# A mixture of experts behind attention and an MLP: products grouped by weight part, later table writes, another seam

## The chip, the cores and the metric

The kernel runs on one core of one Trainium2 chip. The metric is the device time of one execution in microseconds. TensorE is PE in the rows (PEld are its weight loads), VectorE is DVE, ScalarE is ACT, GpSimd is POOL and SyncE is SP.

## What is computed

The reference, cut to what matters. B is 4, 12 heads, 448 positions, 64 per head; x has 1792 rows of 768.

```python
scores = cap * np.tanh((q @ k.T * scale) / cap)
attn = softmax(scores) @ v                         # x: 1792 x 768
h = x @ w_in                                       # 768 -> 2048
x = (h * sigmoid(h)) @ w_out                       # 2048 -> 768
do = x @ w_skip > 0                                # rows that meet an expert
e = argmax(x[do] @ w_gate)                         # one of 8
y[e] = gate_w * (np.maximum(x[e] @ w1[e], 0) @ w2[e])   # 768 -> 1024 -> 768
out = x; out[do] = x[do] + y
```

## The kernel before

All products run in fp32 halves: a number is cut into a high part h and a low part l, and a product is the sum of hi·hi, hi·lo and lo·hi. A high part is a cast on ScalarE, a low part a subtraction on VectorE (or POOL).

Attention fills the first 200 us and the dense MLP the time to about 681; the change does not touch them. Then comes the tail, which is laid out by hand: engines issue in the order in which the Python code records their instructions, and every engine works its own list in order.

The tail begins with the router of the last batch and `group()`, which finds the most loaded expert. Two blocks of few tokens, `fu` and `fv`, have been chosen ahead; their products (`f_h`, `f_y`, L1100) use a quarter of TensorE's columns each and no halves. `f_add` (L1139) sums them on VectorE, `s3_out` (L1077) scatters rows to the output by an indirect DMA on POOL.

The most loaded expert is then worked in blocks of 128 tokens, `gs[0]` to `gs[3]`. For these inputs there are three: block 0 and block 1 are full, and block 2 is "small" (at most 64 rows, where the two halves of the low products share one pass). They share one set of weights. A block is:

- `ids_load` (L889): a DMA reads its 128 token numbers from `table` in DRAM. `own_ids` (L804, L805) corrects the numbers for the last batch, so that blocks 0 and 1 need not wait for the table scatters.
- `x_gather` (L895): an indirect DMA on POOL gathers its rows of x.
- `x_turn` (L972): six transposes on TensorE; `x_split` (L986, L987) cuts the result into halves.
- `h_mm` (L1008): 36 products with w1 (6 parts of the depth, 2 halves of the width, 3 kinds). `h_relu` (L1020), `h_turn` (L1030, L1037, L1038) transpose and cut h.
- `s3_y` (L1051): 48 products with w2; `s3_add` (L1070) adds on VectorE; `s3_out`.

Weights come in six pieces, w1 in three of two rows (1024 columns each) and w2 in three of three, three and two rows (768 columns each). `w_load` (L928) loads a piece on SP, `w_split` and `row_split` (L942, L943) cut it, and `w_next` loads the next expert's piece into the buffer that has come free.

Behind the group come the listed blocks: `cur` and `nxt_`, whose experts, places and number come from `block_list` on VectorE (L811 to L859). `cur` is worked in `body`, the last in `few_body`. Which way the program goes is decided by branches on a register, one for each engine: `more` (L1518), `last` (L1512).

`route_c` scatters the table of token numbers for a batch: four indirect DMAs on POOL (L690). In the kernel before it stands ahead of the gather of block 1, and SP's loads of the later ids wait for it.

The seam is the end of the last group block, where the weights of `cur` must be cut while the block's own y products run. In the kernel before ScalarE casts its pieces (L1481, L942, L1495), VectorE cuts rows 0 to 2, POOL row 3 (L943), and rows 4 and 5 follow the sums; three products of `cur` stand ahead of the branch (`cur.begun = 1`), the rest in `body`.

Of the kernel before, what the change touches and what calls it, by code (L numbers as in the profile page):

```python
# [17 lines left out]
P = 128  # L18
# [4 lines left out]
DM = 768  # L23
# [40 lines left out]
def kernel(  # L64
# [810 lines left out]
    def s_who(idx, re=None):  # L875
        u = Blk()
        u.idx = idx
        u.w1, u.w2, u.raw = {}, {}, {}
        u.begun = 0
        u.small, u.q = False, 1  # L880
        if re is not None:
            u.er = nc.sync.value_load(re, min_val=0, max_val=E - 1)
        return u
# [102 lines left out]
            nc.scalar.copy(h, px)  # L986
            nc.vector.tensor_tensor(l, px, h, op=ALU.subtract)  # L987

    def few(o, t, k, n, h, l):
        both = (o, t[:, k * P : (k + 1) * P], h)  # L990
        rest = (o[:HP], t[:, k * P : k * P + HP], l)
        for i, (o_, t_, w_) in enumerate((both, rest) if k < n - 1 else (rest, both)):
            nc.tensor.matmul(o_, t_, w_, start=(k == 0 and i == 0), stop=(k == n - 1 and i == 1))

    def h_mm(u, nh, ds):
        if nh == 0 and ds[0] == 0:
# [4 lines left out]
        for d in ds:  # L1001
            h, l = u.w1[d]
            o = nh * 512
            if u.small:
                few(u.ph[nh], u.xTh, d, ND, h[:, o : o + 512], l[:, o : o + 512])
                continue
            for x_, w_, st in ((u.xTh, h, 0), (u.xTh, l, 1), (u.xTl, h, 2)):
                nc.tensor.matmul(  # L1008
                    u.ph[nh],
                    x_[:, d * P : (d + 1) * P],  # L1010
                    w_[:, o : o + 512],
                    start=(d == 0 and st == 0),
                    stop=(d == ND - 1 and st == 2),
                )

    def h_relu(u, nh):
        if u.small:
# [22 lines left out]
    def s3_y(u, fs, nhs=(0, 1)):  # L1040
        if 0 in fs:
            u.py = [bank(f"py{nh}") for nh in range(2)]
        for f in fs:
            h, l = u.w2[f]
            for nh in nhs:
                o = nh * HO
                if u.small:
                    few(u.py[nh][:, :HO], u.hTh, f, NF2, h[:, o : o + HO], l[:, o : o + HO])
                    continue
                for x_, w_, st in ((u.hTh, h, 0), (u.hTh, l, 1), (u.hTl, h, 2)):  # L1050
                    nc.tensor.matmul(  # L1051
                        u.py[nh][:, :HO],
                        x_[:, f * P : (f + 1) * P],
                        w_[:, o : o + HO],
                        start=(f == 0 and st == 0),
                        stop=(f == NF2 - 1 and st == 2),
                    )

    def y_out(u):
        i = u.idx % 2  # L1060
# [48 lines left out]
    def f_h(u, ph, ds):  # L1109
        u.ph = ph  # L1110
        r = P // u.q
        for d in ds:
            f_mm(u, ph, u.xT[:, d * r : (d + 1) * r], w_row(u, 1, d), F2, d == 0, d == ND - 1)
# [232 lines left out]
            w_split(u, which, k, eng=nc.gpsimd if (which, k) in ((1, 1), (2, 2)) else nc.vector)  # L1346
            w_next(near, u, which, k)

    def hidden(u, mid=None, mid2=None, both=0):
        h_mm(u, 0, range(u.begun, both or ND))  # L1350
        if both:
            h_mm(u, 1, range(both))
            h_mm(u, 0, range(both, ND))
        h_relu(u, 0)
        if mid is not None:
            mid()
        h_mm(u, 1, range(both, 4))
        h_turn(u, 0)
        if mid2 is not None:
            mid2()  # L1360
        h_mm(u, 1, range(4, ND))
        h_relu(u, 1)

    fu, fv = ahead
# [27 lines left out]
    g0 = s_who(0, regsg[:, :1])  # L1392
    for k in range(3):
        w_load(g0, 1, k)
    w_load(g0, 2, 0)
# [9 lines left out]
    for i in (0, 1):  # L1405
        nc.scalar.copy(w_tile(1, 0, "h")[:, i * F2 : (i + 1) * F2], w_row(g0, 1, i))
    f_relu(fv)
    for k in (1, 2):
        w_load(g0, 2, k)
    py = [ps_y.tile([P, 512], F32, tag="py", name=f"pyf{i}") for i in range(2)]  # L1410
    f_y(fu, py[0], range(6))
    f_hturn(fv, ps_m.tile([P, 512], F32, tag="pm", name="ptf1"), hTf[1:])
    f_y(fu, py[0], (6, 7))
    block_list(*blocks())
    route_c(B - 1)
    own_ids(1, gids[1])
    x_gather(gs[1], xg[1])
    f_add(fu)
    s3_out(fu)
    for i in (0, 1):  # L1420
        row_split(g0, i, done=True)
    for i in (2, 3):
        nc.scalar.copy(w_tile(1, 1, "h")[:, (i - 2) * F2 : (i - 1) * F2], w_row(g0, 1, i))
    f_y(fv, py[1], range(6))
    x_turn(g0)
    f_y(fv, py[1], (6, 7))
    x_split(g0)
    for i in (2, 3):
        row_split(g0, i, done=True)
    for i in (4, 5):  # L1430
        row_split(g0, i)
    w_split(g0, 2, 0)
    f_add(fv)
    s3_out(fv)
    for i in range(2, NG):
        gs.append(ids_load(s_who(i), regsg[:, 1 + i : 2 + i], gids[i]))
    x_gather(gs[2], xg[2])
    total = nc.sync.value_load(regt, min_val=1, max_val=MAXB)

    def listed(i):  # L1440
        u = s_who(i + 1, regs[:, i : i + 1])
        u.real = total > i
        return ids_load(u, regs[:, MAXB + i : MAXB + i + 1], ring["ids"][(i + 2) % 3])

    cur = listed(0)
    x_gather(cur, xg[0])
    w_load(cur, 1, 0)
    for k in range(3):
        w_next((cur,), g0, 1, k)
    w_next((cur,), g0, 2, 0)  # L1450
    nxt_ = listed(1)
# [3 lines left out]
    ng = nc.values_load(regsg[:, 1 + NG :], min_val=0, max_val=2 * NG + 1)  # L1455

    def group_block(i, end, small=False):
# [8 lines left out]
        if end and i != 1:  # L1466
            x_gather(nxt_, xg[1])

        def mid():
            nc.scalar.copy(w_tile(2, 1, "h"), w_raw(g0, 2, 1))  # L1470

        def mid2():
            w_split(u, 2, 1, done=True)
            w_next(pair, g0, 2, 1)

        if i:
            hidden(u)
        else:
            hidden(u, mid, mid2, 2)
        if end:  # L1480
            nc.scalar.copy(w_tile(1, 0, "h"), w_raw(cur, 1, 0))  # L1481
        x_turn(nxt)
        s3_y(u, (0,))
        h_turn(u, 1)
        if i == 0:
            w_split(u, 2, 2)
            w_next(pair, g0, 2, 2)
        x_split(nxt)
        if end:
            w_split(cur, 1, 0, done=True)  # L1490
            w_next(pair, cur, 1, 0)
            row_split(cur, 2)
            row_split(cur, 3, nc.gpsimd)
            w_next(pair, cur, 1, 1)
            nc.scalar.copy(w_tile(1, 2, "h"), w_raw(cur, 1, 2))  # L1495
        s3_y(u, range(1, 4))
        for nh in range(2):
            s3_y(u, range(4, NF2), (nh,))
            s3_add(u, nh)
        if end:  # L1500
            for d in (4, 5):
                row_split(cur, d, done=True)
            w_next(pair, cur, 1, 2)
            h_mm(cur, 0, range(1))
            cur.begun = 1
        s3_out(u)
        if end and i == 1:
            x_gather(nxt_, xg[1])

    def more(i):  # L1510
        def last():
            with tc.If(ng == 2 * i + 3) as half:  # L1512
                group_block(i, True, True)
            with half.Else():
                group_block(i, True)

        if i + 1 < NG:
            with tc.If(ng > 2 * i + 3) as branch:  # L1518
                group_block(i, False)
                if i == 0:  # L1520
                    x_gather(gs[3], xg[3])
                more(i + 1)
            with branch.Else():
                last()
        else:
            last()
# [4 lines left out]
    def body(u, v, alike):  # L1531
# [167 lines left out]
```

## Time and profile before

| what | us |
|---|---|
| three runs: median, lowest, highest | 811.39, 807.75, 1092.96 |
| the profiled execution | 808.66 |
| its span, first to last instruction | 806.9 |
| TensorE matmul busy | 780.7 (97%) |
| VectorE, ScalarE, POOL busy | 471.5, 419.6, 318.0 |
| TensorE's mean granted clock | 0.987 |

A row of a timeline gives the start, the length, the engine, the line, the operation and its operands, and in brackets how long the engine had been idle and what ended that. Line numbers are those of the kernel before. Matmul records overlap: the time of one is read from the distance of two starts. The clock is a share of the full 2.4 GHz.

### The profile page before, as it was taken

Reading aid. Unit: us, or ns where it says so; the run is one execution under the profiler, and the core shown is the slowest. Engines: PE = TensorE matmul, PEld = TensorE weight load, DVE = VectorE, ACT = ScalarE, POOL = GpSimd, SP = SyncE. Lnnn points to the kernel's source line nnn. Section 1 sums busy time; section 2 is a strip of 40 time slices with the busy share of each in tenths; the row PEclk is TensorE's granted clock in tenths of the full one; section 3 lists DMA queues with packets and bytes.
Section 4 is the critical chain, followed back from the end, with each engine's and each line's share of the span. In section 5 each row is a group of like instructions: output and inputs, shape, how many; then the busy total and the mean of one; then the engine's idle time right before and its main releaser. Section 6 shows DMA issues by size and latency. Waiting matters only on the chain. (4 is left out here: it accounts for less than half of the span.)

```text
span 806.9 us, 11338 instructions
## 1 busy us (share of the span) xinstructions
PE 780.7 (97%) x4082; PEld 580.9 (72%) x4082; DVE 471.5 (58%) x678; ACT 419.6 (52%) x584; POOL 318.0 (39%) x218
## 2 busy tenths in 40 slices
PE   7998999999999999999999999999999999899895
PEld 2222222237899999989898999988999896579773
DVE  2799888778888864435424674333664332582451
ACT  6997999993566654443433443333454221252520
POOL 3698988875655545455530220000100000231250
PEclk9999999999999999999999999999999999889998
DMA  7332333341777645677754436965465752876270
GB/s 247 112 131 69 104 116 126 116 149 37 210 209 211 197 130 157 192 221 207 209 171 152 113 101 240 294 208 166 122 207 165 218 144 91 310 257 254 77 242 22
DMA packets 78090, 135.24 MB, mean 168 GB/s; under 512 B 8630, under 2 KB 47926, under 8 KB 78018
## 3 DMA queue, kind: packets, MB, share of 16 engines
q1 hardware_dynamic: 76226, 130.34, 52.0%
q0 software_dynamic: 1504, 4.00, 1.6%
q8 instruction: 38, 0.62, 0.3%
q14 instruction: 34, 0.28, 0.1%
q10 hardware_dynamic: 288, 0.00, 0.0%
HBM read 108.17 MB, written 31.01 MB: 172 GB/s over the span
## 5 line engine op out<-in xcount | busy, mean ns | idle before, releaser
L508 PE MATMUL ph<-x,whi 128*128 128x448 f32 x768 | 217.8, 365 | 0.1
L508 PEld LDWEIGHTS ph<-x,whi 128*128 128x128 f32 x768 | 143.1, 188 | 13.9 <-issue 2.9
L533 PE MATMUL py<-gh,who 128*128 128x448 f32 x384 | 143.3, 373 | 0.0
L533 PE MATMUL py<-gh,wlo 128*128 128x448 f32 x384 | 141.0, 367 | 0.0
L508 PE MATMUL ph<-x,wli 128*128 128x448 f32 x384 | 139.5, 363 | 1.5 <-POOL wli L432 1.5
L533 PE MATMUL py<-gl,who 128*128 128x448 f32 x384 | 140.8, 367 | 0.0
L244 ACT ACTIVATE a<-a,capt 128x896 f32<-128x896 f32 x84 | 87.6, 1043 | 2.8
L243 ACT ACTIVATE a<-psc,tsc 128x896 f32<-128x896 f32 x84 | 83.4, 993 | 8.1 <-PE psc L147 6.1
L204 DVE RECIPROCAL rd<-pden 128x448 f32<-128x448 f32 x24 | 70.9, 2953 | 23.7 <-PE pden L200 23.7
L429 ACT CAST who<-wro 128x512 fp32r<-128x512 f32 x72 | 44.7, 621 | 73.0 <-PE py L533 66.2
L533 PEld LDWEIGHTS py<-gh,who 128*128 128x128 f32 x384 | 72.1, 188 | 10.6 <-ACT who L429 2.2
L525 DVE TENSOR_TENSOR gl<-scr_e,gh 128x448 fp32r<-128x448 f32 x64 | 55.4, 865 | 40.7 <-ACT gh L523 40.0
L523 ACT CAST gh<-scr_e 128x448 fp32r<-128x448 f32 x64 | 36.3, 568 | 80.4 <-DVE scr_e L520 80.4
L533 PEld LDWEIGHTS py<-gh,wlo 128*128 128x128 f32 x384 | 72.1, 188 | 7.1 <-DVE wlo L432 0.4
L508 PEld LDWEIGHTS ph<-x,wli 128*128 128x128 f32 x384 | 72.0, 188 | 6.9 <-POOL wli L432 1.9
L533 PEld LDWEIGHTS py<-gl,who 128*128 128x128 f32 x384 | 72.2, 188 | 6.2
L147 PE MATMUL psc<-q,k 64*128 64x448 f32 x288 | 71.0, 593 | 4.7 <-DMA q<-in_q_dram 4.1
L690 POOL DMA_INDIRECT table<-slotd,si x16 | 17.7, 1107 | 141.9 <-DVE si L680 138.0
L163 POOL TENSOR_TENSOR sm<-sm,a 64x448 f32<-64x448 f32 x48 | 60.4, 1260 | 17.0 <-DVE sm L151 14.6
L176 PE MATMUL pav<-a,vt 128*64 128x448 f32 x288 | 64.6, 562 | 0.0
L432 DVE TENSOR_TENSOR wlo<-wro,who 128x512 fp32r<-128x512 f32 x48 | 33.1, 690 | 53.0 <-ACT who L429 51.1
L154 POOL TENSOR_TENSOR sm<-sm,a 128x896 f32<-128x896 f32 x24 | 51.5, 2145 | 22.1 <-DVE sm L151 10.9
(279 smaller groups left out, 1118.3 us busy)
## 6 DMA issues: line engine op xcount, KB each, us to landing
raw64i<-in_moe_w_in_dram SPq DMA_DIRECT2D x16, 768.0 KB, 5.2
raw64o<-in_moe_w_out_dram SPq DMA_DIRECT2D x24, 512.0 KB, 4.1
wri<-ws_in SPq DMA_DIRECT2D x32, 384.0 KB, 3.1
wro<-ws_out SPq DMA_DIRECT2D x48, 256.0 KB, 3.8
xs<-scr_xo SPq DMA_DIRECT2D x36, 224.0 KB, 4.9
s<-in_moe_w_dram SPq DMA_DIRECT2D x7, 1024.0 KB
ws_in<-wri SPq DMA_DIRECT2D x16, 384.0 KB, 5.7
ws_out<-wro SPq DMA_DIRECT2D x24, 256.0 KB, 4.8
```

What stands on the lines that cost most here:

```text
L147: nc.tensor.matmul(psc[:, j, :S], self.k[r, c * P : (c + 1) * P], self.q[r, :], start=True, stop=True)
L154: nc.gpsimd.tensor_tensor(self.sm, self.sm, self.a[2], op=ALU.add)
L163: nc.gpsimd.tensor_tensor(self.sm[r, q_], self.sm[r, q_], rest[r, o : o + S], op=ALU.add)
L176: nc.tensor.matmul(self.pav[r, :S], self.vt[:, c * 2 + j, :], self.a[c][:, q_], start=(c == 0 and self.hp % 2 == 0), stop=(c == KF - 1 and ...
L204: nc.vector.reciprocal(rd, self.pden[:, :S])
L243: nc.scalar.activation(a.rearrange("p (j s) -> p j s", j=2), self.psc[:, :, :S], AF.Tanh, scale=tsc)
L244: nc.scalar.activation(a, a, AF.Exp, scale=capt)
L429: nc.scalar.copy(self.wh[:, :w], self.wr[:, :w])
L508: nc.tensor.matmul(ph, w_[:, c * P : (c + 1) * P], x_[b, c], start=(n == 0), stop=(n == 3 * ND - 1))
L523: nc.scalar.copy(h, e)
L525: nc.vector.tensor_tensor(l, e, h, op=ALU.subtract)
L533: nc.tensor.matmul(py[:, :S], w_[:, c * P : (c + 1) * P], g_, start=(hf + c + st == 0), stop=(hf == NQ - 1 and c == QC - 1 and st == 2),)
```

## The change

In plain words:

1. `few` becomes `products`, and `h_mm` and `s3_y` take the kinds of products as an argument: "h" for hi·hi, "x" for the low part of the tokens, "l" for the low part of the weights. The products of a block are as many as before; they now run grouped by kind.
2. In front of block 0, its ids are loaded on SP ahead of all but one register load, then the first weight piece, then the ids of block 1; a value that POOL writes behind the gather of block 0 (`gate`) holds back the other five pieces on SP. The list of blocks is made earlier on VectorE.
3. Block 0's h products are issued ahead of the branch, with the cuts of rows 2 to 5 between them; the transposes of block 1's x follow.
4. The table scatters, the loads of the later ids and the gathers of block 2 and of `cur` move behind block 0's h products, all onto POOL (`late_ids`). SP no longer waits for the scatters.
5. `first_block` gives block 0 an order of its own for the w2 cuts and the y products.
6. At the seam ScalarE casts all of w1, VectorE cuts rows 0 and 1 ahead of the sums and rows 2 to 5 in `body` (`late`), POOL cuts none, and eight hi·hi products stand ahead of the branch (`cur.begun = 4`).

```diff
+    def products(small, o, th, tl, ks, n, parts, w_of_k):
+        for part in parts:
+            for k in ks:
+                h, l = w_of_k(k)
+                if not small:
+                    t, w_ = {"h": (th, h), "x": (tl, h), "l": (th, l)}[part]
+                    mms = [(o, t[:, k * P : (k + 1) * P], w_)]
+                else:
+                    both = (o, th[:, k * P : (k + 1) * P], h)
+                    rest = (o[:HP], th[:, k * P : k * P + HP], l)
+                    mms = {"h": [both] if k < n - 1 else [], "x": [], "l": [rest] if k < n - 1 else [rest, both]}[part]
...
-    def hidden(u, mid=None, mid2=None, both=0):
-        h_mm(u, 0, range(u.begun, both or ND))
+    def hidden(u, mid=None, mid2=None):
+        for nh in range(2):
+            h_mm(u, nh, range(u.begun, ND), "h")
+        h_mm(u, 0, range(ND), "x")
+        early = bool(u.small or u.late)
+        if early:
+            h_mm(u, 1, range(ND), "x")
+        h_mm(u, 0, range(ND), "l")
         h_relu(u, 0)
...
-    gs = [ids_load(g0, regsg[:, 1:2], gids[0], nc.scalar)]
-    gs.append(ids_load(s_who(1), regsg[:, 2:3], gids[1], nc.scalar))
+    ids_load(g0, regsg[:, 1:2], gids[0])
+    g0.er = nc.sync.value_load(regsg[:, :1], min_val=0, max_val=E - 1)
+    w_load(g0, 1, 0)
+    ids_load(gs[1], regsg[:, 2:3], gids[1])
...
+    gate = const.tile([1, 1], I32, name="gate")
+    nc.gpsimd.memset(gate, 0)
+    nc.sync.value_load(gate, min_val=0, max_val=0)
...
-    block_list(*blocks())
-    route_c(B - 1)
-    own_ids(1, gids[1])
-    x_gather(gs[1], xg[1])
-    f_add(fu)
+    block_list(*blocks())
+    for d in (0, 1):
+        row_split(g0, d, done=True)
+    f_add(fu)
+    f_y(fv, py[1], range(4))
+    x_turn(g0)
+    f_y(fv, py[1], range(4, NF2))
+    x_split(g0)
+    own_ids(1, gids[1])
+    x_gather(gs[1], xg[1])
...
+    for nh in range(2):
+        h_mm(g0, nh, (0, 1), "h")
+    for nh in range(2):
+        h_mm(g0, nh, (0, 1), "lx")
...
+    h_mm(g0, 1, (4, 5), "l")
+    nc.scalar.copy(h2[:, :DM], w_row(g0, 2, 0))
+    h_relu(g0, 1)
+    f_add(fv)
+    s3_out(fv)
+    x_turn(gs[1])
...
+    def first_block(end):
+        h_turn(u, 1)
+        nc.scalar.copy(h2[:, DM:], w_raw(u, 2, 0)[:, DM:])
+        for nh in range(2):
+            s3_y(u, range(3), (nh,), "hx")
+        w_cut(w_raw(u, 2, 0), h2, l2, done=True)
...
+    def late_ids(end):
+        route_c(B - 1)
+        if not end:
+            for i in range(2, NG):
+                ids_load(gs[i], regsg[:, 1 + i : 2 + i], gids[i], nc.gpsimd)
+            x_gather(gs[2], xg[2])
+        listed(0, cur, nc.gpsimd)
+        x_gather(cur, xg[0])
+        listed(1, nxt_, nc.gpsimd)
...
         if end:
-            w_split(cur, 1, 0, done=True)
+            for k in (1, 2):
+                nc.scalar.copy(w_tile(1, k, "h"), w_raw(cur, 1, k))
+            for d in (0, 1):
+                row_split(cur, d, done=True)
             w_next(pair, cur, 1, 0)
-            row_split(cur, 2)
-            row_split(cur, 3, nc.gpsimd)
...
-            h_mm(cur, 0, range(1))
-            cur.begun = 1
+            cur.begun, cur.late = 4, range(2, ND)
+            for nh in range(2):
+                h_mm(cur, nh, range(cur.begun), "h")
...
+        for d in u.late:
+            row_split(u, d, done=True)
+            if d % 2:
+                w_next(near, u, 1, d // 2)
         splits(u, 2, (0,), near)
```

On SP, in front of block 0: before, the six weight pieces (L928; `s`, `r` and `xraw` are buffers) stand behind one register load, and the ids loads of blocks 0 and 1 stand on ScalarE's queue.

```order
L882 TENSOR_LOAD regsg
L882 ISA x2
L928 ISA
L928 DMA s_5804<-in_moe_w_dram 128x2x1024
L928 ISA
L928 DMA r_4042<-in_moe_w_dram 128x2x1024
```

The same place in the changed kernel:

```order
L889 DMA idg_5924<-table 128x2
L1391 TENSOR_LOAD regsg
L1391 ISA x2
L928 ISA
L928 DMA s_5804<-in_moe_w_dram 128x2x1024
L887 TENSOR_LOAD regsg
L887 ISA x2
L889 ISA
L889 DMA idg_5925<-table 128x2
L1402 TENSOR_LOAD gate
L1402 ISA x2
L928 ISA
```

Two ids loads have come ahead of the weights, and the read of `gate` stands between the first piece and the other five.

On POOL, from the gather of block 0 (`idg_5924`) on, as a difference (`table` is what `route_c` writes, the stores to `out_dram` are those of fu and fv):

```order
 L895 DMA scr_xo<-xs,idg_5924 128x768
+L1401 MEMSET gate 1x1
+L895 DMA xraw<-xs,idg_5925 128x768
+L1070 DMA out_dram<-scr_xt,ids_4037 1792x768
+L1070 DMA out_dram<-scr_xt,ids_4038 1792x768
+L1465 TENSOR_LOAD regsg
+L1559 COMPARE_AND_BRANCH
 L690 DMA table<-slotd,si_5885 15360x2 x4
-L895 DMA xraw<-xs,idg_5925 128x768
-L1077 DMA out_dram<-scr_xt,ids_4037 1792x768
-L1077 DMA out_dram<-scr_xt,ids_4038 1792x768
```

The four scatters have moved behind the gather of block 1, both stores and the branch; behind them now stand, on POOL too, the ids loads of blocks 2 and 3 and then the gather of block 2.

On ScalarE, from the second cut of x of block 0 to its w2 casts (`h_0` and so on are high parts of a piece, `xTh` and `hTh` those of x and h). Before:

```order
L986 CAST xTh_6139<-px_9_5531 128x256
L942 CAST h_2_18_6148<-r_4043 128x1024 x2
L942 CAST h_0_20_6154<-r_4044 128x2304
L1455 TENSOR_LOAD regsg
L1518 COMPARE_AND_BRANCH
L1020 ACTIVATE scr_e<-ph_g 128x512
L1470 CAST h_1_24_6291<-xraw 128x2304
L1037 CAST hTh_6264<-pt_g 128x512
L1020 ACTIVATE scr_e<-ph_g 128x512
L1037 CAST hTh_6264<-pt_g 128x512
L942 CAST h_2_26_6333<-xraw 128x1536
```

In the changed kernel:

```order
L942 CAST h_2_20_6198<-r_4043 128x1024 x2
L1024 ACTIVATE scr_e<-ph_g 128x512
L1041 CAST hTh_6168<-pt_g 128x512
L1457 CAST h_0_22_6232<-r_4044 128x768
L1024 ACTIVATE scr_e<-ph_g 128x512
L1465 TENSOR_LOAD regsg
L1559 COMPARE_AND_BRANCH
L1041 CAST hTh_6168<-pt_g 128x512
L1474 CAST h_0_22_6232<-r_4044 128x1536
L942 CAST h_1_24_6346<-xraw 128x2304
L942 CAST h_2_26_6351<-xraw 128x1536
```

The first w2 piece is cast in two parts, the second of them behind the second cast of h, and the other two pieces follow that.

## Rows read from the trace of the kernel before

**Rows 1.** Stretches: PE, PEld, DVE, ACT, POOL busy us (instructions), granted clock, DMA share, GB/s.

```profile
580.00:600.00 20.00, 20.00 (x102) 18.77 (x101) 13.90 (x34) 10.51 (x17) 5.38 (x5) 1.00 0.52 163
680.00:700.00 20.00, 18.49 (x196) 11.32 (x194) 8.92 (x53) 4.27 (x8) 0.87 (x1) 0.83 0.69 242
700.00:720.00 20.00, 16.95 (x125) 10.78 (x122) 16.61 (x33) 8.43 (x10) 7.78 (x7) 0.83 0.79 255
720.00:740.00 20.00, 20.00 (x110) 18.05 (x109) 9.05 (x11) 6.25 (x10) 6.26 (x5) 1.00 0.98 382
760.00:780.00 20.00, 16.81 (x81) 13.67 (x80) 16.93 (x13) 11.25 (x10) 13.55 (x4) 0.91 0.68 228
```

**Rows 2.** Timeline of PE: start, us, line, out<-in, count, idle before.

```profile
701.64 1.59 PE L1100 MATMUL pyf<-l,hTl 128*32 128x192 f32 x24 [0.43 <-ACT hTl L1125]
...
712.21 0.80 PE L1008 MATMUL ph_g<-h,xTh 128*128 128x512 f32 x1
...
731.08 0.39 PE L1008 MATMUL ph_g<-h,xTh 128*128 128x512 f32 x1
...
739.71 0.82 PE L972 MATMUL px<-ident,xg 128*128 128x128 f32 x6
```

**Rows 3.** Waits, 680 to 714: engine line <- released by: us, times, longest.

```profile
PEld pyf L1100 <- issue: 5.8, 9, 1.3
...
DVE idg L804 <- DMA idg<-table: 5.5, 1, 5.5
```

**Rows 4.** Timeline of POOL.

```profile
699.13 1.04 POOL L895 DMA_INDIRECT scr_xo<-xs,idg  x1 [104.28 <-DMA idg<-table]
...
704.27 0.95 POOL L690 DMA_INDIRECT table<-slotd,si  x1 [0.30 <-issue]
...
733.51 1.03 POOL L895 DMA_INDIRECT scr_xo<-xs,idg  x1 [0.30 <-issue]
...
751.58 1.03 POOL L895 DMA_INDIRECT xraw<-xs,ids  x1 [0.30 <-PE ph_g L993]
```

**Rows 5.** Timeline of PE at the seam.

```profile
767.35 0.49 PE L1008 MATMUL ph_g<-h,xTh 128*128 128x512 f32 x1 [3.07 <-DVE scr_xt L1070]
...
768.58 0.63 PE L1008 MATMUL ph_g<-l,xTh 128*128 128x512 f32 x1
...
772.01 0.39 PE L1008 MATMUL ph_g<-l,xTh 128*128 128x512 f32 x1
```

**Rows 6.** Line L1512 on the engines' queues: ns min/median/max, first and last start.

```profile
L1512 PEldq COMPARE_BRANCH  x2: 83/1852/3622, 749.5 to 763.0; - x2
```

**Rows 7.** Timeline of ACT.

```profile
773.22 1.47 ACT L942 CAST h<-xraw 128x1536 fp32r<-128x1536 f32 x1
```

**Rows 8.** Timeline of DVE, and the POOL row beside its last.

```profile
706.40 1.69 DVE L1139 SCALAR_TENSOR_TENSOR scr_xt<-pyf,ids,xg 32x192 f32<-32x192 f32 x4 [2.02 <-remote]
...
721.73 0.69 DVE L1038 TENSOR_TENSOR hTl<-pt_g,hTh 128x512 fp32r<-128x512 f32 x1 [1.04 <-ACT hTh L1037]
...
722.34 2.55 DVE L943 TENSOR_TENSOR l<-xraw,h 128x2304 fp32r<-128x2304 f32 x1
...
760.66 5.62 DVE L943 TENSOR_TENSOR l<-s,h 128x2048 fp32r<-128x2048 f32 x2
...
777.06 3.67 DVE L943 TENSOR_TENSOR l<-r,h 128x2304 fp32r<-128x2304 f32 x1
...
774.83 3.48 POOL L943 TENSOR_TENSOR l<-xraw,h 128x1536 fp32r<-128x1536 f32 x1 [0.51 <-ACT h L942]
```

**Rows 9.** Timeline of SP's queue, and its issues with median us to landing.

```profile
711.03 1.53 SPq L889 DMA_DIRECT2D idg<-table  x2
...
idg<-table SPq DMA_DIRECT2D x2, 1.0 KB, 3.3
```

**Rows 10.** DMA busy tenths, 751.5 to 759.5; software queue, 736.3 to 738.6.

```profile
DMA  0497991009779765240000000000000000000000
...
q0 software_dynamic: 110, 0.58, 61.2%
```

More of the change, by code (lines that the diff above doesn't have):

```diff
@@ L878, in s_who @@
         u.w1, u.w2, u.raw = {}, {}, {}
-        u.begun = 0
+        u.begun, u.late = 0, ()
         u.small, u.q = False, 1
@@ L987, in x_split, with h_mm @@
             nc.vector.tensor_tensor(l, px, h, op=ALU.subtract)
[L989 to L996, printed above, removed]
+    def products(small, o, th, tl, ks, n, parts, w_of_k):
[9 more added lines that the diff above has]
+                    mms = {"h": [both] if k < n - 1 else [], "x": [], "l": [rest] if k < n - 1 else [rest, both]}[part]
+                for i, (o_, t_, w_) in enumerate(mms):
+                    nc.tensor.matmul(
+                        o_,
+                        t_,
+                        w_,
+                        start=(k == 0 and part == "h"),
+                        stop=(k == n - 1 and part == "l" and i == len(mms) - 1),
+                    )
+    def h_mm(u, nh, ds, parts):
+        if nh == 0 and ds[0] == 0 and parts[0] == "h":
             u.ph = [bank(f"ph{i}") for i in range(2)]
@@ L1000, in h_mm @@
             u.hTl = slot("eb", "hTl", [P, F2], F32R)
[L1001 to L1014, printed above, removed]
+        cs = slice(nh * 512, (nh + 1) * 512)
+        w = lambda d: (u.w1[d][0][:, cs], u.w1[d][1][:, cs])
+        products(u.small, u.ph[nh], u.xTh, u.xTl, ds, ND, parts, w)
     def h_relu(u, nh):
@@ L1038, in h_turn, with s3_y @@
             nc.vector.tensor_tensor(u.hTl[:, cs], u.pt, u.hTh[:, cs], op=ALU.subtract)
-    def s3_y(u, fs, nhs=(0, 1)):
-        if 0 in fs:
+    def s3_y(u, fs, nhs=(0, 1), parts="hxl"):
+        if 0 in fs and 0 in nhs and parts[0] == "h":
             u.py = [bank(f"py{nh}") for nh in range(2)]
[L1043 to L1057, printed above, removed]
+        for nh in nhs:
+            cs = slice(nh * HO, (nh + 1) * HO)
+            w = lambda f: (u.w2[f][0][:, cs], u.w2[f][1][:, cs])
+            products(u.small, u.py[nh][:, :HO], u.hTh, u.hTl, fs, NF2, parts, w)
     def y_out(u):
@@ L1356, in hidden @@
             mid()
-        h_mm(u, 1, range(both, 4))
+        h_mm(u, 1, *((range(4), "l") if early else (range(ND), "x")))
         h_turn(u, 0)
@@ L1360, in hidden @@
             mid2()
-        h_mm(u, 1, range(4, ND))
+        h_mm(u, 1, range(4, ND) if early else range(ND), "l")
         h_relu(u, 1)
@@ L1424, with who_of, listed @@
[L1424 to L1432, printed above, removed]
+    total = nc.sync.value_load(regt, min_val=1, max_val=MAXB)
+    def who_of(i):
+        u = s_who(i + 1, regs[:, i : i + 1])
+        u.real = total > i
+        return u
+    def listed(i, u=None, eng=None):
+        return ids_load(u or who_of(i), regs[:, MAXB + i : MAXB + i + 1], ring["ids"][(i + 2) % 3], eng)
@@ L1433 @@
+    h_turn(g0, 0)
+    h_mm(g0, 1, (4, 5), "l")
+    h2, l2 = (w_tile(2, 0, c) for c in "hl")
+    g0.w2.update({i: tuple(t[:, i * DM : (i + 1) * DM] for t in (h2, l2)) for i in range(3)})
+    nc.scalar.copy(h2[:, :DM], w_row(g0, 2, 0))
+    h_relu(g0, 1)
     f_add(fv)
     s3_out(fv)
[L1435 to L1443, printed above, removed]
@@ L1455 @@
     ng = nc.values_load(regsg[:, 1 + NG :], min_val=0, max_val=2 * NG + 1)
+    def first_block(end):
+        u, pair = g0, (cur, nxt_)
+        if end:
+            x_gather(nxt_, xg[1])
+            x_turn(cur)
+        h_turn(u, 1)
[3 more added lines that the diff above has]
+        w_cut(w_raw(u, 2, 0), h2, l2, done=True)
+        w_next(pair, u, 2, 0)
+        w_split(u, 2, 1)
+        w_next(pair, u, 2, 1)
+        w_split(u, 2, 2)
+        w_next(pair, u, 2, 2)
+        for nh in range(2):
+            s3_y(u, range(3), (nh,), "l")
+        for fs in (range(3, 6), range(6, NF2)):
+            for nh in range(2):
+                s3_y(u, fs, (nh,), "hx")
+        x_split(cur if end else gs[1])
+    def late_ids(end):
[7 more added lines that the diff above has]
+        listed(1, nxt_, nc.gpsimd)
     def group_block(i, end, small=False):
```

91 lines of the change are left out of this document (44 added, 47 removed).

## The prediction

> **What bounds the kernel now.** I read the busy time by stretch first, then the waits, then the engines' timelines at the two places where TensorE is not busy. The program has one core. Its dense part is full (the page's slices stand at 9), so the reader should look only at the tail, where the diff works. [Rows 1] give five stretches of 20 us, one of them from the dense part: TensorE misses 1.5 us before 700, 3.1 us in 700 to 720, and 3.2 us in 760 to 780, and the granted clock there is 0.83, 0.83 and 0.91, so part of what counts as busy runs at the lower of the two levels (1.2 GHz). From 720 to 740 TensorE is full at 1.00, as it is in the dense part. Whatever the change gains must come out of these two places; nothing else is open.
>
> The first place is the way into block 0 [rows 2]. The products of the second few-token block (fv) start at 701.64 with 24 in 1.59 us, 66 ns each; the rest of its 64 take until 712.21, where block 0 begins. [Rows 3] say why: the weight loads of these products stood for "issue", nine times, 5.8 us in all, the longest 1.3. VectorE's sum of the first few-token block (fu), whose products stand ahead of 701.64, waits until 706.40, "remote" [rows 8]. TensorE is fed slowly there, a trickle whose cause the trace does not name. Beside it stand the four table scatters on POOL (the last at 704.27, 0.95 long with 0.30 ahead of it [rows 4], so 1.25 each), a DMA under load (0.79 here and 0.98 in the next stretch), and the late ids: VectorE waited 5.5 us for those of block 0 [rows 3].
>
> The second place is the seam after the small block [rows 5]: 3.07 us without a product, put down to the VectorE sum L1070. But TensorE's own queue holds the better row [rows 6]: its branch L1512 took up to 3622 ns, at 763.0. Behind the gap a product is 0.63 long (768.58) where a later one is 0.39 (772.01): up to 0.24 more for each.
>
> **The front, step by step.** (a) Ids before weights, gate, gather earlier. The gather of block 0 stood at 699.13 [rows 4] because of those ids. With one weight load ahead of it and the others held behind the gate, it should be issued some 4 us sooner. This takes the wait for x off the path and fills VectorE's idle 5.5 us with the block list; neither is the bound as long as the trickle stands. (b) The scatters leave this stretch. If that, or the earlier list, or the lighter load ends the trickle, fv takes 64 x 66 ns = 4.2 us from 701.64 and the transposes of x 0.8 (0.82 at 739.71 [rows 2]): block 0 begins at 706.6, less some 0.4 where the two overlap: 706.2 against 712.21, a gain of 6.0. Block 0's first products then need not run at 1.2 GHz, as those at 712.21 did (0.80 for a record that is 0.39 later): block 0 took 18.87 to 731.08 [rows 2], block 1's like work 18.1, so 0.8 more. If the trickle stays, (a) and (b) give nothing. The bounds of this term are 0 and 6.8; I take 6.8: in 580 to 600 POOL had five such jobs and TensorE stayed full, in 720 to 740 the DMA was fuller and TensorE stayed full [rows 1], so that only the crowd of all three explains the trickle, and the crowd goes.
>
> (c) The first block's new order. The products are the same 84, regrouped: by itself nothing. But ScalarE now has, between the second activation and the y products of f1, the turn's cast and a cast of 1536 columns, which took 1.47 in [rows 7]: the turn's transposes and its cast (512 columns, 0.5 by the same rate), then 1.5, with a few products to cover them. I price it at 2.0 (between 0.5 and 2.7). The 2304-wide low part follows on VectorE, 2.55 in [rows 8], against 18 products of some 0.2 each (a block's 18.1 less the 8.6 up to its transposes at 739.71, over 48), of which part has run by then: 0.6 more. Together 2.6 lost. The cover in the kernel before was that these casts stood beside the h products, and it is gone.
>
> (d) The table chain. SP's ids loads stood at 711.03, 5.8 after the last scatter (704.27 + 0.95) [rows 4, 9]; nobody on TensorE waited, since x of block 2 was wanted only at 739.71 [rows 2], 8.6 after block 1 began. Now the chain starts behind VectorE's sum of fv, which stands behind the first low part of h. With block 0 at 706.2 that low part ends at 715.6 (it ended 10.2 after the start before, 721.73 + 0.69 [rows 8], less the 0.8 at the lower clock), the sum at 717.3 (1.69), the store that POOL must issue first at some 718.5, a branch, then four scatters of 1.25 until 723.9, 5.8 to the ids loads (729.7), which POOL now issues itself, and 3.3 until they have landed [rows 9], in which the second load is issued too: the gather at 733.0. A gather takes 3.7 us on an idle DMA (issued 751.58; of the 40 slices of 0.2 us from 751.5 the last busy one is the 19th) to 5.1 (issued 733.51, its packets until 738.6) [rows 4, 10]: 736.7 to 738.1. Block 1 begins at 706.2 + 18.1 + 2.6 = 726.9 and wants it at 735.5. So TensorE waits 1.2 to 2.6 at block 1's transposes. With landing times half as long it waits nothing, and with a gather as slow as the first may have been (issued 699.13, used at 709.29 or earlier) some 6. I take 2.0. What is queued behind it is all of TensorE; POOL's queue behind it (stores, the list's gathers) has slack until the seam.
>
> **The seam.** Both remaining w1 casts move ahead on ScalarE, POOL's split of row 3 goes, two 1024-wide splits stay before the sums and four go behind them, and eight products instead of three stand before the branch. The gap of 3.07 ended at 767.35, so the small block's y products and three of 0.23 (8.6 over 36 and a turn) ended at 764.28, the y products alone at 763.6. TensorE's queue met the branch at 763.0, held until then by VectorE's first low part, which began at 760.66 [rows 8]. Now it waits there for ScalarE's cast of rows 2 and 3 alone, by my count 761.9 (1.9 for 2048 columns by [rows 7], behind two others). Taken at 3.6 us the branch ends at 765.5; with some 0.7 to the first product, 766.2. Eight products end at 765.3: a gap of 1.0 instead of 3.07, and perhaps none of the eight products at 0.63, 1.9 more. The h phase would end 4.0 earlier. VectorE's two splits took 5.62 where POOL's stood beside them; rows 0 and 1 alone take 2.3 (1024 columns at the rate of 2.55 for 2304 are 1.13), the sums then end at about 766.0, and rows 2 to 5 cost 4.6 behind them, just ahead of the low products that want them, so that hides.
>
> Not all of it reaches the end. The next wait is the low part of w2's second piece: 3.67 from 777.06 beside POOL's split (774.83, 3.48), where an undisturbed one took 2.55 [rows 8]. 774.83 + 3.48 = 778.31, and 2.4 later it ends: it stood until POOL was through. After the change POOL's split starts only 1.4 earlier (its cast follows the first activation), so this part is ready at 779.4 instead of 780.7. I book 1.1 of the 4.0. The Trainium skill's page "SBUF — State Buffer", section "SBUF: two separate sides", calls the port pair that VectorE and GpSimd share an exclusive lock, held for a whole instruction, for a VectorE operation with two SBUF inputs. By that rule the 4.0 is capped as said, because the change leaves this pair of splits as it was; without it the split would run from 773.2 to 775.8 and some 3.5 would stay. The row of 3.67 sides with the rule: 778.31 and 2.42 behind it, where 2.55 is an undisturbed split.
>
> **Sum.** -6.8 + 2.6 + 2.0 - 1.1 = -3.3 us. Against the profiled execution, 808.66 (span 806.9 and 1.8 around it), that is 805.4. The median shown is 811.39 and the lowest run 807.75, so a run may stand 3 above this with nothing behind it.
>
> **Rivals.** First, slower: the trickle belongs to the stretch's code or to the load of weights, and stays. The gate does not lessen the bytes, and 64 short products are still fetched under a full DMA; that speaks for it. Against it: 720 to 740 is as loaded and TensorE is full there. Then the 6.8 is gone while (c) and (d) are paid: 808.66 + 2.6 + 2.0 - 1.1 = 812.2. It decides as soon as more than 3.3 of the 6.8 is lost. Second, both gains are kept: casts and table come in time and the seam's 4.0 is whole: 808.66 - 6.8 - 4.0 = 797.9. For it speaks that (c) and (d) are my counts, not rows; against it row 777.06. Third, the gaps only move: a wait of 2 in block 0 and another in block 1 are each followed by eight products at 1.2 GHz as at the seam (1.6 to 1.9 each), so 805.4 + 3.2 = 808.6, no change. Here the regrouping does nothing, since the tail stays bound by the same chains.
>
> **How the numbers follow.** A measurement of this kernel can tell about 2%, 16 us, from no change. The idle time of [rows 1] in the two places is 7.8, with a lower clock in part of the rest, so no case reaches that bound by itself. Chances: forecast 0.45 (own range 802 to 808), trickle stays 0.25, both gains 0.2, gaps only move 0.1. The range goes from the second rival to the first with a bit for the run, 798 to 813. Faster by over 2% 0.03 (an unseen gain on top of both), slower 0.03 (both waits long, 6 and 2.7, and the trickle), within 2% 0.94.
>
> **What would show it.** Right: the products of fv in one run of about 4 us, block 0's first product near 706; a wait of ScalarE's cast and of VectorE's low part in front of the y products of block 0; a wait at block 1's transposes for a DMA; the seam's gap about 1 us with products of 0.39 behind it; and the 2304-wide split still about 3.5. Wrong: "issue" waits of 5 us at fv's products, wherever they stand; no wait at block 1's transposes; or a time outside 798 to 813.

## The result and the profile after

The changed kernel takes 815.89 us (median of ten runs, 813.63 to 818.16), the kernel before 808.75. The ratio is 1.0109 with an interval of 1.0087 to 1.0131, about 8.8 us slower; the medians differ by 7.1. The ratio is one of fast runs, so one run of the kernel before, of 1092.96 us, is not in it. The forecast was 805.4, the range 798 to 813. Both the sign and the range were missed. The profiled execution took 815.06 with a span of 813.5.

Read first the stretches, with the columns of [rows 1] (busy of PE, PEld, DVE, ACT, POOL, then clock, DMA share, GB/s):

```profile
680.00:700.00 20.00, 18.48 (x191) 11.66 (x194) 11.84 (x64) 3.02 (x7) 1.13 (x2) 0.91 0.46 150
...
700.00:720.00 20.00, 17.25 (x165) 12.80 (x158) 14.25 (x26) 11.98 (x16) 4.55 (x4) 1.00 1.00 385
...
720.00:740.00 20.00, 17.81 (x83) 15.60 (x81) 8.53 (x8) 4.87 (x7) 8.62 (x7) 0.91 0.85 268
...
740.00:760.00 20.00, 15.92 (x73) 14.30 (x74) 2.86 (x5) 1.86 (x4) 5.72 (x6) 0.83 0.36 119
```

In the kernel before, 720 to 740 was full [rows 1] and 740 to 760 nearly so:

```profile
740.00:760.00 20.00, 19.54 (x116) 17.26 (x115) 3.99 (x8) 6.85 (x13) 2.05 (x2) 1.00 0.13 44
```

Now these two miss 2.2 and 4.1 us, with a clock of 0.91 and 0.83. In 700 to 720 TensorE still misses 2.8 us, but the clock is 1.00 where it was 0.83. TensorE's timeline names the places:

```profile
701.77 1.48 PE L1093 MATMUL pyfpl<-l,hTl 128*32 128x192 f32 x32
...
705.43 1.20 PE L1002 MATMUL ph_g<-h,xTh 128*128 128x512 f32 x4
...
713.73 0.66 PE L1034 MATMUL pt_g<-ident,scr_e 128*128 128x128 f32 x4 [0.30 <-ACT scr_e L1024]
...
716.29 0.66 PE L1034 MATMUL pt_g<-ident,scr_e 128*128 128x128 f32 x4 [0.59 <-ACT scr_e L1024]
...
718.99 0.61 PE L1002 MATMUL py_g<-h,hTh 128*128 128x384 f32 x2 [1.87 <-ACT h L1474]
...
728.97 2.92 PE L1002 MATMUL ph_g<-h,xTh 128*128 128x512 f32 x12
...
742.29 1.54 PE L972 MATMUL px<-ident,xg 128*128 128x128 f32 x6 [4.48 <-DMA xg<-xs,idg]
...
743.95 0.52 PE L1002 MATMUL py_g<-h,hTl 128*128 128x384 f32 x1
```

These answer to [rows 2]. The products of fv run without a break (32 in 1.48 us, the other 32 behind block 0's transposes) and block 0 begins at 705.43. But block 0 waits 0.30, 0.59 and 1.87 us for ScalarE, and block 1's transposes wait 4.48 us for the gather of block 2. The record at 743.95 is 0.52 long where an undisturbed y product is 0.34: 1.2 GHz. Two narrow stretches show that clock, 0.57 and 0.50, behind either wait:

```profile
720.00:724.00 4.00, 4.00 (x15) 3.66 (x14) 4.00 (x3) 3.09 (x4) 3.64 (x2) 0.57 1.03 404
...
742.00:747.00 5.00, 4.71 (x18) 4.62 (x19) 0.00 (x0) 0.36 (x1) 3.42 (x4) 0.50 0.37 126
```

POOL's timeline shows why the gather was late (compare [rows 4]):

```profile
717.61 0.89 POOL L1070 DMA_INDIRECT out_dram<-scr_xt,ids  x1 [7.82 <-DVE scr_xt L1132]
...
718.81 0.94 POOL L690 DMA_INDIRECT table<-slotd,si  x1 [0.32 <-issue]
...
720.06 2.29 POOL L690 DMA_INDIRECT table<-slotd,si  x1 [0.30 <-issue]
...
722.65 2.17 POOL L690 DMA_INDIRECT table<-slotd,si  x1 [0.30 <-issue]
...
725.12 1.37 POOL L690 DMA_INDIRECT table<-slotd,si  x1 [0.30 <-issue]
...
735.21 0.60 POOL L889 DMA_DIRECT2D idg<-table  x1 [8.72 <-DMA table<-slotd,si]
...
738.33 1.08 POOL L895 DMA_INDIRECT xg<-xs,idg  x1 [1.35 <-DMA idg<-table]
```

The store of fv at 717.61 is followed by four scatters, two of them 2.29 and 2.17 long and one 1.37 instead of 0.95; the ids load waits 8.72 for the table, and the gather is issued at 738.33. The same places set side by side, each counted from the first own_ids product (L799) of its own profile so that what lies ahead drops out:

| us after that product | before | before again | after | tab1 | cast | best |
|---|---|---|---|---|---|---|
| block 0 begins | 21.26 | 18.21 | 12.13 | 10.95 | 12.13 | 12.07 |
| block 1 begins | 40.13 | 36.67 | 35.67 | 36.01 | 32.44 | 33.01 |
| block 2 begins | 58.83 | 55.66 | 61.84 | 55.49 | 61.96 | 51.95 |
| `cur` begins | 72.46 | 69.30 | 76.83 | 70.01 | 76.78 | 66.69 |
| last block's f_h | 91.68 | 88.55 | 94.81 | 88.09 | 94.89 | 82.59 |

"Before again" is a second profile of the kernel before; the other columns are experiments. Against it the change gains 6.1 in front, loses 5.1 in block 0, 7.2 in block 1 and 1.4 in block 2, and gains 1.3 at the seam: +6.3.

### The profile page after: what moved, and what is told of

The parts are those of the page before. It is cut to its first block, busy times and chain, and to the rows that moved or that the text cites. A ratio compares the mean times of both kernels' runs of the same rounds, so it can differ in the third digit from the quotient of the medians.

```text
span 813.5 us, 11339 instructions
## 1 busy us (share of the span) xinstructions
PE 780.9 (96%) x4082; PEld 581.2 (71%) x4082; DVE 471.8 (58%) x680; ACT 420.4 (52%) x584; POOL 311.1 (38%) x222
## 4 chain that ended last, share of the span: by engine, by line
PE 78%; DMA 5%; issue 5%; DVE 5%; POOL 4%; ACT 1%; POOLq 0%; SPq 0%; another core or an unknown queue 0%; ACTq 0%
PE py L533 29%; PE ph L508 28%; PE pav L176 5%; PE psc L147 5%; DMA out_dram<-scr_xt,idg 5%; PE pden L200 2%; DVE rd L204 2%; PE psc L239 1%; PE pt L545 1%; PE pav L188 1%; PE pl L567 1%; PE ph_g L1002 1%; ACT a L243 1%; DVE sm L151 1%; POOL sm L163 1%
## 5 line engine op out<-in xcount | busy, mean ns | idle before, releaser
L163 POOL TENSOR_TENSOR sm<-sm,a 64x448 f32<-64x448 f32 x48 | 60.4, 1260 | 16.9 <-DVE sm L151 14.5
```

Of the source, the lines that this page charges most:

```text
L163: nc.gpsimd.tensor_tensor(self.sm[r, q_], self.sm[r, q_], rest[r, o : o + S], op=ALU.add)
```

## Experiments

**Is it the table chain?** tab1 moves one line.

```diff
+    x_gather(gs[1], xg[1])
+    route_c(B - 1)
...
     def late_ids(end):
-        route_c(B - 1)
```

> The changed kernel with one line moved: the four table scatters stand behind the gather of block 1 instead of behind block 0's h products; ids loads and the gather of block 2 stay where they are. Late chain (theory): the table is written some 9 us sooner, the gather of block 2 is issued near 724 instead of 738, the 4.5 us wait at block 1's transposes and the half clock behind it go, about 7 us less: near 809. Rival, the gather itself is slow under the load of weights: the wait stays at 3 or more, near 815. Rival, scatters anywhere near the front slow TensorE's issue again: the wait goes but block 0's products show issue waits of some 5 us, near 814.

Measured: 807.09, ratio 1.0018 (1.0004 to 1.0032). The wait is nearly gone, and no half clock follows it:

```profile
738.93 0.87 PE L972 MATMUL px<-ident,xg 128*128 128x128 f32 x6 [0.40 <-DMA xg<-xs,idg]
...
749.18 2.08 PE L1002 MATMUL ph_g<-h,xTh 128*128 128x512 f32 x8 [0.56 <-issue]
```

The theory holds: 7.4 us of the ratio's 8.8 hang on where four scatters stand. Part of the expectation missed: the gather was issued at 732.11 and not near 724, because on POOL the ids loads still stood behind the store of fv (722.55, 2.96 long). It came just in time.

**Does the cast cost by itself?** cast replaces the two part casts and the cut by a whole `w_split(g0, 2, 0)` ahead of `h_relu(g0, 0)`.

```diff
     h_mm(g0, 0, range(2, ND), "l")
+    w_split(g0, 2, 0)
     h_relu(g0, 0)
...
-    nc.scalar.copy(h2[:, :DM], w_row(g0, 2, 0))
...
-        nc.scalar.copy(h2[:, DM:], w_raw(u, 2, 0)[:, DM:])
...
-        w_cut(w_raw(u, 2, 0), h2, l2, done=True)
```

> The changed kernel with the first w2 piece cast whole and cut ahead of block 0's first activation, where ScalarE and VectorE stand idle for 3 us; nothing else moves. Theory: the 1.87 us wait for the cast and the half clock behind it go and block 0 takes about 4 us less, but the table chain is where it was, so block 1's transposes wait that much longer: the time stays within 1 us of 815.9. Rival, the two losses are independent: 4 us less, near 812.

Measured: 813.71, ratio 1.0092 (1.0069 to 1.0114), and in its profile:

```profile
724.63 2.92 PE L1002 MATMUL ph_g<-h,xTh 128*128 128x512 f32 x12
...
742.15 1.54 PE L972 MATMUL px<-ident,xg 128*128 128x128 f32 x6 [8.69 <-DMA xg<-xs,idg]
```

Block 0 takes 20.3 us instead of 23.5, and the wait behind it grows from 4.48 to 8.69: the gather sets the end, so the tail is as long as before (94.89 against 94.81). The time fell by 1.4 (by the ratio) to 2.2 us (by the medians), and the two intervals overlap. The median lies between the theory and the rival, so the time alone does not decide; the profile does, for the theory.

**Do VectorE and POOL block each other at the seam?** k2dve:

```diff
         def mid2():
             w_split(u, 2, 1, done=True)
             w_next(near, u, 2, 1)
+            w_split(u, 2, 2, done=True)
+            w_next(near, u, 2, 2)
...
         def mid():
-            splits(u, 2, (2,), near)
+            nc.scalar.copy(w_tile(2, 2, "h"), w_raw(u, 2, 2))
```

> The changed kernel with POOL's cut of the third w2 piece of the listed block given to VectorE, behind the second piece's. If the two engines block each other: VectorE's cut of the second piece takes 2.5 us instead of 4.9, the 1.85 us wait in front of its low products goes, 1.9 us less, near 814. Rival, the wait is only a matter of order on VectorE: the cut still ends near 786 and the time is the same or longer by the 1.8 of the third cut.

Measured: 813.62, ratio 1.0083 (1.0061 to 1.0106). In the changed kernel, VectorE with the POOL row beside it:

```profile
781.20 4.91 DVE L943 TENSOR_TENSOR l<-r,h 128x2304 fp32r<-128x2304 f32 x1
```
```profile
780.21 3.48 POOL L943 TENSOR_TENSOR l<-xraw,h 128x1536 fp32r<-128x1536 f32 x1 [6.81 <-ACT h L942]
```

and in k2dve:

```profile
782.23 2.55 DVE L943 TENSOR_TENSOR l<-r,h 128x2304 fp32r<-128x2304 f32 x1
...
784.69 1.75 DVE L943 TENSOR_TENSOR l<-xraw,h 128x1536 fp32r<-128x1536 f32 x1
```

4.91 became 2.55, and from `cur`'s start to the last block's f_h it took 16.26 instead of 17.98: the expected 1.7 to 1.9.

**What held block 0 in the kernel before?** tab0 puts `route_c` right behind the gate; bscat moves it in the kernel before behind fu's store; nogate is tab1 without the gate's three lines; again is the kernel before.

> The changed kernel with the four table scatters right behind the gather of block 0 and the gate, so that they run while fv's short products are issued, as in the kernel before. If the scatters make the trickle: issue waits of about 5 us at fv's products return, block 0 begins near 711 of the profile instead of 705.4, and with the wait at block 1 gone the time is near 814. Rival, the trickle came from the load of weights or from the place of the list: block 0 still begins near 705.5, near 809.

> The kernel before with the four table scatters behind fu's store instead of ahead of block 1's gather; nothing else moves. If the scatters fed the trickle: the issue waits at fv's products (5.8 us of weight loads) go and block 0 begins some 5 us sooner after the first own_ids product than the 21.3 of before. Rival, they do not (the profile with the scatters put back in the changed kernel began block 0 12.1 after that product): the trickle stays and block 0 begins at 21 or later.

> The kernel with the scatters behind block 1's gather, and without the gate: the five weight pieces follow the ids on SP at once. If the weights under way make the trickle: issue waits at fv's products return and block 0 begins 15 or more after the first own_ids product instead of 11 to 12, or x of block 0 lands late and its transposes wait. Rival, the gate is not what ended it: block 0 begins at 11 to 12.

> The kernel before, profiled a second time, for the time at which its dense part ends. The four profiles of the changed kernel and its variants have the first own_ids product at 692.2 to 694.1, the one of before at 690.95. If the dense part differs only from run to run, this one lies between 690 and 694 with no order; if it is earlier in the kernel before as such, it lies at 691 or below.

Measured: tab0 809.49 (ratio 1.0044, 1.0026 to 1.0062), block 0 at 12.07; bscat 809.8 (one run), block 0 at 18.74; nogate 804.48 (one run), block 0 at 12.12; again 805.64 (one run), block 0 at 18.21. bscat met neither expectation: fv's issue waits are down to 1.0 us, but a wait of 3.73 for the gather stands in their place. Neither the scatters alone nor the gate decide. The second profile of the kernel before says what does:

```profile
698.41 2.16 PE L1100 MATMUL pyf<-l,hTl 128*32 128x192 f32 x48 [0.35 <-DVE base L811]
...
706.23 1.54 PE L972 MATMUL px<-ident,scr_xo 128*128 128x128 f32 x6 [5.67 <-DMA scr_xo<-xs,idg]
...
709.14 0.68 PE L1008 MATMUL ph_g<-h,xTh 128*128 128x512 f32 x1
```

Here the first 48 of fv's 64 products take 2.16 us, with no trickle at all, and block 0's transposes then wait 5.67 for the gather of x. So it is in b32, b64 and b256 of the next question, the kernel before with one unread tile: waits of 3.56, 4.89 and 5.72, block 0 at 17.07, 18.34 and 19.59. The trickle of [rows 2, 3] belongs to one execution, in which it covered this wait. What the change gains in front is the earlier ids and gather: the gather is issued 2.6 us behind the first own_ids product (695.86) instead of 8.2 (699.13). The trickle came back mildly in one more profile (best0, where block 0 began at 15.06). In both, the scatters stand ahead of block 1's gather on POOL. They stand there in five other profiles without a trickle (again, b32, b64, b256, tab0), and none of the eleven that have them later shows one. So the scatters alone do not make it; whether they are part of it is not shown, and its cause stays open.

**Why does the untouched dense part end later?** In the profiles, the first own_ids product stands at 690.95, 690.93, 690.43 and 689.52 (before, again, bscat, nogate) and at 693.30, 693.69, 693.12, 692.19, 694.10 and 691.59 (after, tab1, tab0, cast, k2dve, best). The first four lack the gate's tile. It is allocated in the first pool, and by the programs' addresses its 32 bytes move over 500 later tiles. b32, b64 and b256 add to the kernel before such a tile of 4, 64 and 256 bytes, which POOL writes and nobody reads; gate64 makes the gate's tile 64 bytes; gate_eb takes it from the pool of the tail, which moves two.

```diff
     x_gather(g0, xg[3])
+    gate = const.tile([1, 1], I32, name="gate")
+    nc.gpsimd.memset(gate, 0)
```

> The kernel before with one more tile in the pool that lies ahead of the others: the 4-byte tile of the gate, written once by POOL and read by nobody. It moves some 500 later tiles in SBUF up by 32 bytes; all addresses that were multiples of 64 no longer are. If that is what makes the dense part longer: the first own_ids product comes 2 to 3 us later than 690.9 and the time is 2 to 3 us above before. Rival, the dense part differs for another reason or by chance: the ratio to before is 1.000.

> The same with a tile of 64 bytes, which moves the later tiles by 64. If alignment is the cause: as before, ratio 1.000, the first own_ids product at 690 to 691. If it is any move of the tiles, or the added write on POOL: as the tile of 4 bytes.

> The changed kernel with the gate's tile 64 bytes wide instead of 4, nothing else. If alignment costs the changed kernel its dense part: 2 to 3 us less than the changed kernel, ratio to before near 1.008, the first own_ids product at 690 to 691. Rival: ratio as the changed kernel, 1.011, and that product at 692 to 694.

> The changed kernel with the gate's 4-byte tile taken from the pool of the tail, so that all other tiles but two lie where they lie in the kernel before. If moving the tiles is what lengthens the untouched dense part: the first own_ids product at 689.5 to 691 as in the four profiles without the tile, and some 2.4 us less than the changed kernel: ratio to before near 1.008. Rival, the dense part differs for another reason that comes with the change: 692 or later, ratio 1.011.

> The kernel before with an unread tile of 256 bytes in front. If what counts is where the tiles lie to a boundary of 128 or 256 bytes: dense part as before, 690 to 691, ratio 1.000. If any move costs: 692, ratio 1.002 to 1.003 as with 32 and 64 bytes.

| run | tiles moved by | first own_ids product | ratio to before | 512-byte packet, mean ns |
|---|---|---|---|---|
| b32 | 32 | 691.81 | 1.0029 (1.0013 to 1.0046) | 30 |
| b64 | 64 | 692.32 | 1.0018 (0.9998 to 1.0037) | 30 |
| b256 | 256 | 689.52 | 1.0004 (0.9978 to 1.0029) | 28 |
| gate64 | 64 | 694.20 | 1.0121 (1.0094 to 1.0148) | 30 |
| gate_eb | 0 | 691.12 | 1.0086 (1.0051 to 1.0122) | 28 |

The last column is the mean of the packets of 512 bytes between 200 and 680 us, some 26,000 in each trace; it is 28 in every profile with tiles unmoved or moved by 256, and 30 in every other. My first guess, a boundary of 64, fell with b64 and gate64; a larger one fits. Each interval alone is too wide for 2 us, and one later profile (best_eb, tiles unmoved) has the product at 694.72, so the cost is pointed to, not shown; the packets' length is shown.

**Does a repair of all three beat both kernels?** best combines tab1, cast and k2dve and moves the ids loads of blocks 2 and 3 ahead of fv's store; best64 and best_eb change only the gate's tile; best0 is best_eb with the scatters behind the gate.

> The changed kernel with all three repairs: scatters behind block 1's gather and the ids of blocks 2 and 3 behind them ahead of fv's store; the first w2 piece cast and cut ahead of block 0's first activation; the listed block's third w2 piece cut by VectorE. If the three losses are what the change paid: no wait at block 1's transposes, block 0 in about 20.3 us, no wait for the second w2 piece's low part, some 10 us less in the tail than before, and about 6 us less than before in all: near 800. Rival, the losses only move on to the next wait: near 806.

> The kernel with the three repairs, its gate's tile 64 bytes wide. If alignment is a cost of its own: 1 to 3 us less than the version with 4 bytes (ratio 0.994), near 0.991. Rival: 0.994.

> The kernel with the three repairs and the gate's tile in the tail's pool. If the move of the tiles is a cost of its own: the first own_ids product at 689.5 to 691, some 2 us less than the version with the tile in front: ratio to before near 0.991. Rival: 0.994 to 0.998 and a product at 692.

> The repaired version with the four scatters in POOL's idle time right behind the gather of block 0, so that the table chain has 7 us more: best and its variants run either near 800 or near 807, and the one profile of the slow kind has two scatters of 2.0 and 3.3 us, the gather of block 2 at 732.4 and a wait of 3.7 us for it. If the late chain is what splits them: no wait at block 1's transposes, runs near 799 without a second group at 807, ratio to before near 0.991. Rival, the split has another cause: some runs stay near 807.

Measured: best 801.13, ratio 0.9940 (0.9917 to 0.9964); best64 802.52, 0.9981 (0.9955 to 1.0007); best_eb 804.84, 0.9965 (0.9934 to 0.9996); best0 803.95, 0.9958 (0.9927 to 0.9988). A version faster than both exists: best is 0.6% (0.4 to 0.8) below the kernel before, by five runs; best_eb and best0 are below it too, while the interval of best64 reaches 1.0007. In best, TensorE behind block 0 keeps its clock:

```profile
716.00:724.00 8.00, 7.29 (x42) 6.98 (x41) 6.99 (x9) 4.17 (x5) 2.08 (x3) 1.00 0.94 232
...
724.00:744.00 20.00, 19.36 (x105) 17.43 (x104) 4.72 (x8) 3.65 (x7) 5.44 (x7) 1.00 0.84 325
```

The tile's place did not show in these medians (best is the best of them), and the runs of the last three, twelve each, spread from 799 to 811, where the five of best lay between 800.7 and 801.3. The profile of best_eb has the wait for block 2's gather again, 3.74 us, behind scatters of 2.03 and 3.27; best0 took that chain off the edge (gather at 718.25) and still spread from 800 to 809. So the late chain is not all of the spread, and what else it is stays open.

## Why the prediction was wrong

The step that failed most is (d), the table chain: it was booked at 2.0 and cost 7.2, because the scatters and the table's landing took longer behind block 0's products than in the front, and because the lower clock behind a wait was left out of (c) and (d).

- **(a), (b), the front.** Booked at 6.8; 6.1 against the second profile of before, 9.1 against the first. The size was nearly right, and its reason wrong: I wrote that the wait for x was not the bound as long as the trickle stands. The trickle was gone in "again", and there the wait for x was the bound. So the size was luck in part: the forecast removed a trickle, the change removed a wait. The rival "trickle stays" did not happen.
- **(c), the first block.** Booked at 2.6, measured 5.1. The wait for ScalarE was named rightly and is 2.8 in all (0.30, 0.59 and 1.87) where I took 2.0; the 0.6 for VectorE's low part did not come. What failed is that I priced only the waits; TensorE then ran at 0.57 for 4 us, which is 1.7 more. The other 0.6 has no row of its own.
- **(d), the table chain.** Booked at 2.0, measured 7.2 in block 1. The chain was followed rightly to the store (718.5 forecast with a start 0.8 later, 717.61 to 718.50 measured). Then "four scatters of 1.25 until 723.9" failed: they ended at 726.5, and the table took 8.7 to the ids load where I took 5.8. TensorE waited 4.48, and 5 us at 0.50 followed, 2.5 more. What held the scatters was VectorE, at its cuts:

```profile
718.97 2.56 DVE L943 TENSOR_TENSOR l<-r,h 128x2304 fp32r<-128x2304 f32 x1 [0.68 <-ACT h L1474]
...
721.45 4.22 DVE L943 TENSOR_TENSOR l<-xraw,h 128x2304 fp32r<-128x2304 f32 x2
```

The second row is two cuts, the first of them until 724.00. The last three scatters began inside one cut each and ended 0.82 us behind its end: at 722.35, 724.82 and 726.49, behind 721.53, 724.00 and 725.67. It is so in every trace: of the table scatters in the tail, 24 begin inside a cut, more than 0.05 us behind its start and more than 0.2 ahead of its end, and all 24 end 0.81 to 0.86 behind the cut; the other 48 take 0.94 to 1.27. In tab1 the scatter at 707.62 took 1.94 in this way; the one at 709.86 began just ahead of a cut (709.99) and the one at 711.13 in the last 0.1 us of one, and they took 0.96 and 0.94. The load of the DMA does not separate them: its share was 1.03 in before too (700.4 to 705.3), beside four scatters of 0.94 to 0.98. The Trainium skill's page "SBUF — State Buffer", section "SBUF: two separate sides", warns that a VectorE operation in a mode that takes two ports keeps GpSimd from writing the descriptors of a DMA that POOL issues; to an operation with two SBUF inputs, as these cuts are, it gives the lock only against a GpSimd operation that reads SBUF. The rows show that such a cut does hold a scatter; by which of these ways they do not show. This makes 3.0 us of the chain's delay (2.29, 2.17 and 1.37 against 0.95 each). The table's longer landing makes 2.9, and why it took 8.7 here and 5.8 in before stays open (6.6 in best, 7.1 in best_eb).
- **The seam.** Booked at 1.1, measured 1.3. The cap by the pair of cuts was right: POOL's ended at 783.69, VectorE's took 4.91 and ended 2.42 later, as in before, and TensorE waited 1.85 for it. k2dve shows it from the other side. The gap of 3.07 shrank to 0.49, where I had 1.0. Behind neither wait did the clock fall; behind the longer one the stretches read:

```profile
772.64 1.17 PE L1002 MATMUL ph_g<-h,xTh 128*128 128x512 f32 x4 [0.49 <-ACT h L942]
...
786.16 0.44 PE L1002 MATMUL py_g<-l,hTh 128*128 128x384 f32 x1 [1.85 <-DVE l L943]
```
```profile
784.00:786.00 2.00, 0.31 (x2) 0.00 (x0) 2.00 (x1) 0.00 (x0) 2.00 (x1) 1.00 0.90 345
786.00:788.00 2.00, 1.84 (x10) 1.69 (x10) 0.71 (x2) 0.00 (x0) 0.97 (x1) 1.00 0.51 89
```

- **Not in the sum.** 1.4 at the start of block 2, where TensorE waits 0.66 and 1.13 for "issue" behind a branch (L1559, up to 3635 ns), against 0.46 in before and 0.7 in again; and some 2.4 in the dense part. The branch and the products behind it:

```profile
L1559 PEldq COMPARE_BRANCH  x3: 65/95/3635, 715.4 to 751.2; - x3
```
```profile
755.14 2.06 PE L1002 MATMUL ph_g<-h,xTh 128*128 128x512 f32 x8 [0.66 <-issue]
...
758.33 0.73 PE L1002 MATMUL ph_g<-h,xTh 128*128 128x512 f32 x2 [1.13 <-issue]
```

The branch itself is not the difference: L1518 at the same place took 3412 ns in before and 3655 in again. Block 2 takes 14.5 to 15.0 in every profile of the changed kernel and its variants and 13.6 in before, again, b32, b64 and b256, so the 1.4 comes with the change; what makes the second wait stays open.

With both the sum is -6.1 + 5.1 + 7.2 + 1.4 - 1.3 + 2.4 = 8.7, against 8.8 by the ratio. That they are so close is luck in part: it is a sum of single profiles, whose executions differ by 9.4 (815.06 and 805.64), and the medians differ by 7.1.

- **The rivals.** Nearly half of what came (1.7 and 2.5 of 8.8) was the third: the waits in block 0 and in block 1 each drew a stretch at 1.2 GHz, the wait of 1.85 at the seam did not. I gave it 0.1 and took it as an alternative to the forecast, though the seam of [rows 5] had shown it behind its wait of 3.07. Added to the forecast's own waits it gives 808.6, and with the chain's longer end, 6 instead of 2.0, 812.6: the sign was within reach of my own numbers, the whole loss was not.
- **The range.** It took the waits at their booked sizes. The case that I named under "slower" (the trickle, waits of 2.7 and 6) gives 808.66 + 2.7 + 6 - 1.1 = 816.3: outside the range, and still within 2%. In (d) I took the last busy slice of [rows 10] for the 19th; it is the 18th, so the shorter gather is 3.5 us and not 3.7, which changes little.

## What to carry to other kernels

A wait that a change adds costs its length and can cost half as much again in products at the lower clock behind it (1.7 behind 2.8, 2.5 behind 4.48 here, nothing behind the 1.85 at the seam); both belong in the sum. Work that is moved off the front must be followed to its next reader with the load it meets there: four scatters that nobody had waited for became the longest chain of the tail, held by VectorE's cuts and by a slower landing. And one profile can show a bound that is not there in the next; a second profile of the kernel before would have shown the wait for x at once.

## What the runs showed that I had not expected

- POOL's table scatter, begun while VectorE runs one of the cuts, ends 0.81 to 0.86 us behind the end of that cut, so that one of 0.95 became one of 2.29.
- A 4-byte tile in the first pool moves over 500 tiles by 32 bytes, and packets of 512 bytes then take 30 ns on the mean instead of 28, in all ten profiles with tiles moved by 32 or 64 and in none of the eight others.
- The place of the scatters did not set the start of block 0 in the changed kernel: with them right behind the gate (tab0) block 0 began at 12.07, with them behind fv's store (after) at 12.13. In best0, with them behind the gate, it began at 15.06.
